# A decode block on one core: the first load issued in two parts, and seven transfers of rows in place of eight

## The chip, the cores and the metric

The kernel runs on one core of a Trainium2 chip. The metric is the device time of one execution in microseconds (us). The kernel before has a median of 213.9 us over three runs (213.82 to 213.99).

One execution was also recorded by the hardware profiler, and the profile shown here is of that one. Its engines are TensorE (PE, with its weight loads as PEld), VectorE (DVE), ScalarE (ACT), GpSimd (POOL) and SyncE (SP). SP does no arithmetic here: it issues transfers. A "q" behind an engine's name (SPq, ACTq) marks its instruction sequencer, which is what issues a transfer.

## The reference: attention over a cache, then a two-layer network

The block is one decode step for four tokens (B = 4) of width D = 448. What is computed, cut to what matters:

```python
def _A_ref(x, k_cache, v_cache, wq, wo):            # 16 query heads, 8 key heads, head size 256
    W = min(4096, max(256, Sk // 4))                # the last 1024 of 4096 cached positions
    q = (x @ wq).reshape(B, Sq, Hq, Dh) ...
    k = jnp.repeat(k_cache[:, :, Sk - W:, :], rep, axis=1)
    v = jnp.repeat(v_cache[:, :, Sk - W:, :], rep, axis=1)
    scores = jnp.einsum("bhqd,bhkd->bhqk", q, k) * (Dh ** -0.5)
    p = _softmax(scores, axis=-1)
    o = jnp.einsum("bhqk,bhkd->bhqd", p, v)
    return o ... @ wo
def _B_ref(x, w1, b1, w2, b2):                      # 448 -> 1792 -> 448
    y = _layernorm(x, axis=-1)
    h = _gelu(jnp.einsum("bsd,df->bsf", y, w1) + b1)
    return jnp.einsum("bsf,fd->bsd", h, w2) + b2

h = x + _A_ref(_layernorm(x, axis=-1), A_k_cache, A_v_cache, A_wq, A_wo)
h2 = h + _B_ref(_layernorm(h, axis=-1), B_w1, B_b1, B_w2, B_b2)
```

All data is float32. The keys and values of the last 1024 positions, for 8 heads and 4 tokens, are most of the 88 MB that are read from HBM.

## The kernel before

**Layout and staging.** The host packs everything that belongs together into arrays of 128 rows, one row for each SBUF partition, so that one transfer fills one stretch of all 128 partitions. Three large buffers form a ring (`slot`, line 50). The transfers fill them in turn: `t0` (first head), then `ta`, `tb`, `tc`, `td` for heads 0 to 2 and again for heads 3 to 5, and `te0` to `te2` for the last heads and the weights of the second layer. A buffer is filled again as soon as the work on its former content is done; that wait stands at the issue of the transfer.

**Who issues.** SP issues every load of these arrays, in program order, through `load` (line 53; the issue is on line 57). A load without a list of pieces is one transfer. ACT issues the small transfers of `rows` into the tile `rs` (lines 302 and 319). The three engines PE, SP and ACT run in the order in which the kernel's text names their instructions; nothing reorders them.

**The start.** Lines 259 to 267 issue the first loads: `wq0` (the query weights of head 0 and the transposed `x`: 128 rows of 7232 bytes) into the beginning of `t0`, then `k0` (keys of head 0 and most of the query weights of head 1) behind it, then two small transfers of 32 rows of 2048 bytes each into `wq1_last` (line 265). After these SP goes on to `ta` and `tb`. Lines 268 to 276 compute the first layer norm from `xT`, which lies in the `wq0` part; line 277 projects the first query; line 279 computes the first scores, which need `k0`.

**The rows.** The tile `rs` holds `x` and the two biases for the second half of the block. They are laid out in four groups of four partitions (0, 32, 64 and 96 onward), and for each group the kernel before issues two transfers, 256 columns and 448 columns wide (1 KB and 1.75 KB on each partition): four transfers at line 302 for groups 0 and 1, four at line 319 for groups 2 and 3. The first use of `rs` is line 400, near the end.

**The end.** The last loads are the pieces of `w2` (line 337). Line 463 multiplies with the first of them, line 473 with the rest, line 479 adds up, and line 480 writes the result.

Of the kernel before, what the change touches and what calls it, by code (L numbers as in the profile page):

```python
# [15 lines left out]
B, D = 4, 448  # L16
# [4 lines left out]
P = 128  # L21
H = P // 2
ND = 4
NKC = W // P
NFC = F // P
FQ = F // 4
# [3 lines left out]
WEIGHTS = 4 * D  # L30
# [5 lines left out]
def block_kernel(ctx: ExitStack, tc, rows, wq0, k0, wq1, la, lb, lc, ld, k7, vo, w1, w2, out):  # L36
    nc = tc.nc
# [12 lines left out]
    def slot(name):  # L50
        return ring.tile([P, SLOT], F32, tag="r", name=name)

    def load(t, at, src, pieces=None):
        dst = t[:, at : at + src.shape[-1]]
        at = 0
        for n in pieces or (src.shape[-1],):
            nc.sync.dma_start(dst[:, at : at + n], src[:, at : at + n])  # L57
            at += n
        return dst

    def cut(t, sizes):
        parts, at = [], 0
        for n in sizes:
            parts.append(t[:, at : at + n])
            at += n
        return parts


    def wq_parts(t, last=None):
        parts = [(a, yT[:, a, :], slice(0, 512), t[:, a * 512 : (a + 1) * 512]) for a in range(3)]  # L70
        if last is not None:
            return parts + [(3, yT[:H, 3, :], slice(0, 512), last)]
        for i in range(2):
            parts.append((3, yT[:, 3 + i, :], slice(i * 2 * P, (i + 1) * 2 * P), t[:, 3 * 512 :]))
        return parts


    def keys(t):
        return t.rearrange("p (c b k) -> p c b k", c=2, b=B)

    def chunks(t):
        v = t.rearrange("p (c b d) -> p c b d", b=B, d=DH)
        return [v[:, c : c + 2] for c in range(0, v.shape[1], 2)]
# [65 lines left out]
    def project_q(g, parts):  # L149
        pq = ps_m.tile([P, 512], F32, tag="m", name=f"pq{g}")  # L150
        for j, y, cols, w in parts:
            nc.tensor.matmul(pq[j * Q : (j + 1) * Q, cols], y, w, start=True, stop=True)  # L152
        qs = work.tile([P, 512], F32, tag="qs", name=f"qs{g}")
        nc.scalar.copy(qs, pq)  # L154

        pt = ps_m.tile([P, 2 * REP, P], F32, tag="m", name=f"pqt{g}")
        for i in range(2 * REP):
            nc.tensor.transpose(pt[:, i, :], qs[:, i * P : (i + 1) * P], ident)  # L158
        sm = work.tile([P, 2 * REP, B], F32, tag="sm", name=f"sm{g}")
        nc.vector.tensor_reduce(  # L160
            sm, pt.rearrange("p i (j q) -> p i q j", j=4)[:, :, :B, :], axis=AX.X, op=ALU.add
        )

        src = sm.rearrange("p (r c) b -> p c b r", r=REP)
        for i in range(2):
            nc.vector.tensor_copy(qT[g % 2][:, :, :, i * REP : (i + 1) * REP], src)

    def scores_half(g, h, kt):
        s = ps_s.tile([P, 512], F32, tag="s", name=f"s{g}_{h}")
        for c in range(2):  # L170
            for b in range(B):
                nc.tensor.matmul(  # L172
                    s[b * Q : (b + 1) * Q, :], qT[g % 2][:, c, b, :], kt[:, c, b, :],
                    start=(c == 0), stop=(c == 1),
                )
        m = work.tile([P, 1], F32, tag=f"mx{h}", name=f"mx{g}_{h}")
        nc.vector.reduce_max(m, s, axis=AX.X)  # L177
        return s, m

    def softmax(g, parts):  # L180
        halves, mx = zip(*parts)
        nm = work.tile([P, 1], F32, tag="nm", name=f"nm{g}")
        nc.vector.tensor_max(nm, mx[0], mx[1])
        nc.vector.tensor_scalar_mul(nm, nm, -SCALE)  # L184
        p = once.tile([P, 2 * 512], F32, tag="p", name=f"p{g}")
        sums = work.tile([P, 2], F32, tag="sums", name=f"sums{g}")
        for h in range(2):
            nc.scalar.activation(  # L188
                p[:, h * 512 : (h + 1) * 512], halves[h], AF.Exp, bias=nm, scale=SCALE,
                accum_out=sums[:, h : h + 1],  # L190
            )
        rec = work.tile([P, 1], F32, tag=f"rec{g % 3}", name=f"rec{g}")
        nc.vector.tensor_add(rec, sums[:, 0:1], sums[:, 1:2])
        nc.vector.reciprocal(rec, rec)
        return p, rec

    def scores(g, kt):
        return [scores_half(g, h, kt[h]) for h in range(2)]

    def transpose_p(g, p):  # L200
        for h in range(2):
            pt = ps_t.tile([P, 4, P], F32, tag="t", name=f"ppt{g}_{h}")
            for c in range(4):
                nc.tensor.transpose(pt[:, c, :], p[:, (4 * h + c) * P : (4 * h + c + 1) * P], ident)  # L204

            src = pt.rearrange("p (c i) (b q) -> p c i b q", i=2, b=B)
            for i in range(2):
                nc.vector.tensor_copy(
                    pT[g % 2][:, 2 * h : 2 * h + 2, :, i * REP : (i + 1) * REP], src[:, :, i, :, :REP]
                )  # L210


    def values(g, vt, po, pairs=range(NKC // 2)):
        for c in pairs:
            for b in range(B):
                nc.tensor.matmul(  # L216
                    po[b * Q : (b + 1) * Q], pT[g % 2][:, c, b, :], vt[c][:, :, b, :],
                    start=(c == 0), stop=(c == NKC // 2 - 1),
                )
# [35 lines left out]
    def po_tile(g, pool=ps_o, tag="o"):  # L255
        return pool.tile([P, 2, DH], F32, tag=tag, name=f"po{g}")


    t = slot("t0")
    wqt, xT = cut(load(t, 0, wq0), (WEIGHTS, ND * B))  # L260
    wqt = wq_parts(wqt)
    xT = xT.rearrange("p (a b) -> p a b", a=ND)
    ka, kb, wqt1 = cut(load(t, WEIGHTS + ND * B, k0), (HALF, HALF, 3 * 512))
# [17 lines left out]
    p, rec = softmax(0, parts)  # L281
    transpose_p(0, p)

    def finish(g, po, rec, wt):
        transposed_output(g, po, rec)
        add_output(g, output_weights(wt))

    for g in (0, 3):
        ka, kb, wqt, va = cut(load(slot(f"ta{g}"), 0, la[g // 3]), (HALF, HALF, WEIGHTS, HALF))
        parts = scores(g + 1, [keys(ka), keys(kb)])  # L290
        project_q(g + 2, wq_parts(wqt))
        p, rec_next = softmax(g + 1, parts)
        transpose_p(g + 1, p)
        po = po_tile(g)
        va = chunks(va)
        values(g, va, po, range(0, 2))

        vb, wot, ka, kb = cut(load(slot(f"tb{g}"), 0, lb[g // 3]), (HALF, WEIGHTS, HALF, HALF))
        if g == 0:
            for j in range(2):  # L300
                for cols in (slice(0, 2 * P), slice(2 * P, 2 * P + FQ)):
                    nc.scalar.dma_start(rs[j * Q : j * Q + B, cols], rows[j][:, cols])
        values(g, va + chunks(vb), po, range(2, 4))
        p, rec_then = softmax(g + 2, scores(g + 2, [keys(ka), keys(kb)]))
        finish(g, po, rec, wot)
        transpose_p(g + 2, p)

        wqt, v, wot, ka = cut(load(slot(f"tc{g}"), 0, lc[g // 3]), (WEIGHTS, CACHE, WEIGHTS, HALF))
        project_q(g + 3, wq_parts(wqt))
        po = po_tile(g + 1)  # L310
        values(g + 1, chunks(v), po)
        first_half = scores_half(g + 3, 0, keys(ka))
        finish(g + 1, po, rec_next, wot)

        kb, wqt, v, wot = cut(load(slot(f"td{g}"), 0, ld[g // 3]), (HALF, WEIGHTS, CACHE, WEIGHTS))
        if g == 0:
            for j in range(2, 4):
                for cols in (slice(0, 2 * P), slice(2 * P, 2 * P + FQ)):
                    nc.scalar.dma_start(rs[j * Q : j * Q + B, cols], rows[j][:, cols])
        parts = [first_half, scores_half(g + 3, 1, keys(kb))]  # L320
        project_q(g + 4, wq_parts(wqt))
        p, rec = softmax(g + 3, parts)
        transpose_p(g + 3, p)
        po = po_tile(g + 2)
        values(g + 2, chunks(v), po)
        finish(g + 2, po, rec_then, wot)
# [11 lines left out]
    p, rec_last = softmax(g + 1, scores(g + 1, kt))  # L338
# [122 lines left out]
    for c in range(first):  # L461
        j, m = c % 4, Q if c < 4 else B
# [90 lines left out]
```

## Time and profile before

| What | Value |
|---|---|
| median of 3 runs | 213.9 us (213.82 to 213.99) |
| profiled execution, its own time | 213.97 us |
| its span, first to last instruction | 212.2 us |
| read from HBM | 88.26 MB, 416 GB/s over the span |
| PE busy | 133.4 us (63% of the span) |
| DVE, ACT, POOL busy | 38.4, 21.2, 5.6 us |
| transfers of SP's queue (q1) | 3248 packets, 88.29 MB |
| transfers of ACT's queue (q10) | 64 packets, 0.05 MB |

The profiled execution took 213.97 us, of which 1.8 us lie outside its span; it stands 0.07 us above the median. Times within the span are counted from the first instruction. A packet is one row of a transfer on one of the core's 16 DMA engines, or the 4-byte write that ends a transfer on an engine. The view by windows counts a packet, with all its bytes and all its time, in the window in which it starts, so that single windows can show more than the whole rate.

### The profile page before, as it was taken

The page shows a single profiled execution, that of the slowest core. Times are in us where ns is not written, and L with a number is a line of the kernel's source. Part 1 is how long each engine was busy: PE and PEld are TensorE (multiplying, and loading weights), DVE is VectorE, ACT ScalarE, POOL GpSimd, SP SyncE. Part 2 cuts the span into 40 slices and gives each one's busy share as a digit, 9 for nine tenths or more (in the row PEclk, how much of TensorE's full clock was granted, in tenths as well). Part 3 has the DMA queues.
Part 4 walks back from the last instruction along what each step waited for, and adds up shares of the span by engine and source line. Part 5 has one row for each costly group of instructions (what it writes and reads, how often), then busy time and mean ns, then how long its engine had stood idle before and what let it go on. Part 6 is the DMA issues. An engine that isn't in the chain of part 4 may idle for free.

```text
span 212.2 us, 2296 instructions
## 1 busy us (share of the span) xinstructions
PE 133.4 (63%) x970; PEld 47.1 (22%) x970; DVE 38.4 (18%) x167; ACT 21.2 (10%) x52; POOL 5.6 (3%) x17
## 2 busy tenths in 40 slices
PE   0457815841960597188398088138917879978994
PEld 0322201310220221032123022012202322324432
DVE  1420310410230003022014013100200323122310
ACT  2010300300020100030003002001000302010311
POOL 6100000000000000000000000000000000000200
PEclk9999995995896559579969759855885999999999
DMA  7999898999999999999999999999989999999992
GB/s 292 426 396 534 350 499 361 481 416 467 397 419 482 407 420 420 467 393 457 428 425 467 422 407 482 407 431 407 479 349 463 442 399 424 432 393 439 424 398 77
DMA packets 3321, 88.46 MB, mean 417 GB/s; under 512 B 400, under 2 KB 688, under 8 KB 1392
## 3 DMA queue, kind: packets, MB, share of 16 engines
q1 hardware_dynamic: 3248, 88.29, 97.1%
q8 instruction: 7, 0.11, 0.2%
q10 hardware_dynamic: 64, 0.05, 0.1%
q14 instruction: 2, 0.02, 0.0%
HBM read 88.26 MB, written 0.07 MB: 416 GB/s over the span
## 4 chain that ended last, share of the span: by engine, by line
DMA 78%; PE 16%; SPq 2%; DVE 1%; issue 1%; ACT 1%; ACTq 0%
DMA tb<-lb 23%; DMA ta<-la 21%; DMA td<-ld 20%; DMA te<-w 14%; PE s L172 6%; PE po L216 4%; SPq L57 2%; PE ppt L204 1%; PE acc L245 1%; PE pq L152 1%; PE pa L463 1%; PE py L473 1%; SPq L265 1%; PE pqt L158 1%; ACT qs L154 1%
## 5 line engine op out<-in xcount | busy, mean ns | idle before, releaser
L177 DVE TENSOR_REDUCE mx<-s 128x1 f32<-128x512 f32 x16 | 11.1, 691 | 56.1 <-PE s L172 56.1
L172 PE MATMUL s<-ta,qT 128*32 128x512 f32 x64 | 10.7, 830 | 10.1 <-DMA ta<-la 10.1
L154 ACT COPY qs<-pq 128x512 f32<-128x512 f32 x8 | 4.7, 585 | 116.2 <-PE pq L152 116.2
L188 ACT ACTIVATE p<-s,nm 128x512 f32<-128x512 f32 x16 | 10.9, 688 | 46.4 <-DVE nm L184 46.4
L233 DVE TENSOR_SCALAR o<-po,rec 128x512 f32<-128x512 f32 x8 | 6.0, 750 | 50.5 <-PE po L216 50.5
L216 PE MATMUL po<-tb,pT 128*32 128x512 f32 x32 | 6.9, 1019 | 12.9 <-DMA tb<-lb 12.9
L152 PE MATMUL pq<-tc,yT 128*32 128x512 f32 (+1 forms) x20 | 3.9, 891 | 16.8 <-DMA tc<-lc 16.8
L172 PE MATMUL s<-td,qT 128*32 128x512 f32 x32 | 6.9, 1016 | 10.7 <-DMA td<-ld 10.7
L216 PE MATMUL po<-tc,pT 128*32 128x512 f32 x64 | 11.9, 909 | 0.0
L204 PE MATMUL ppt<-ident,p 128*128 128x128 f32 x64 | 10.5, 287 | 0.7 <-ACT p L188 0.4
L158 PE MATMUL pqt<-ident,qs 128*128 128x128 f32 x32 | 6.6, 340 | 6.0 <-ACT qs L154 6.0
L204 PEld LDWEIGHTS ppt<-ident,p 128*128 128x128 f32 x64 | 6.7, 141 | 6.3 <-ACT p L188 6.3
L160 DVE TENSOR_REDUCE sm<-pqt 128x16 f32<-128x64 f32 x8 | 1.8, 224 | 34.4 <-PE pqt L158 34.4
L216 PE MATMUL po<-te,pT 128*32 128x512 f32 x64 | 7.5, 595 | 0.6 <-DMA te<-vo 0.6
L172 PE MATMUL s<-tb,qT 128*32 128x512 f32 x64 | 7.4, 601 | 0.0
L216 PE MATMUL po<-td,pT 128*32 128x512 f32 x64 | 7.3, 595 | 0.0
L237 PE MATMUL pot<-ident,o 128*128 128x128 f32 x32 | 5.3, 287 | 2.7 <-DVE o L233 2.7
L345 PE MATMUL warm<-idle 128*32 128x512 bf16 x22 | 6.8, 382 | 0.0
L158 PEld LDWEIGHTS pqt<-ident,qs 128*128 128x128 f32 x32 | 4.2, 169 | 11.4 <-ACT qs L154 9.7
L172 PE MATMUL s<-t,qT 128*32 128x512 f32 x32 | 5.3, 829 | 2.0 <-DMA t<-k 2.0
L172 PEld LDWEIGHTS s<-ta,qT 128*32 128x32 f32 x64 | 2.6, 147 | 17.5 <-issue 13.5
L146 POOL TENSOR_TENSOR r<-ve_r,mhalf 128x1 f32<-128x1 f32 x2 | 1.1, 542 | 190.3 <-DVE ve_r L145 190.3
(129 smaller groups left out, 112.1 us busy)
## 6 DMA issues: line engine op xcount, KB each, us to landing
tc<-lc SPq DMA_DIRECT2D x2, 7936.0 KB
td<-ld SPq DMA_DIRECT2D x2, 7936.0 KB
ta<-la SPq DMA_DIRECT2D x2, 7040.0 KB
tb<-lb SPq DMA_DIRECT2D x2, 7040.0 KB
te<-vo SPq DMA_DIRECT2D x1, 4992.0 KB
t<-k SPq DMA_DIRECT2D x1, 4864.0 KB
te<-k SPq DMA_DIRECT2D x1, 4096.0 KB
te<-vo SPq DMA_DIRECT2D x1, 3072.0 KB
```

Of the source, the lines that this page charges most:

```text
L57: nc.sync.dma_start(dst[:, at : at + n], src[:, at : at + n])
L152: nc.tensor.matmul(pq[j * Q : (j + 1) * Q, cols], y, w, start=True, stop=True)
L154: nc.scalar.copy(qs, pq)
L158: nc.tensor.transpose(pt[:, i, :], qs[:, i * P : (i + 1) * P], ident)
L172: nc.tensor.matmul(s[b * Q : (b + 1) * Q, :], qT[g % 2][:, c, b, :], kt[:, c, b, :], start=(c == 0), stop=(c == 1),)
L177: nc.vector.reduce_max(m, s, axis=AX.X)
L188: nc.scalar.activation(p[:, h * 512 : (h + 1) * 512], halves[h], AF.Exp, bias=nm, scale=SCALE, accum_out=sums[:, h : h + 1],)
L204: nc.tensor.transpose(pt[:, c, :], p[:, (4 * h + c) * P : (4 * h + c + 1) * P], ident)
L216: nc.tensor.matmul(po[b * Q : (b + 1) * Q], pT[g % 2][:, c, b, :], vt[c][:, :, b, :], start=(c == 0), stop=(c == NKC // 2 - 1),)
L233: nc.vector.tensor_scalar_mul(o, po, rec)
L237: nc.tensor.transpose(pt[:, i, c], o[:, i, c * P : (c + 1) * P], ident)
L345: nc.tensor.matmul(warm[:Q], idle[:, :Q], idle, start=True, stop=True)
```

## The change

The first load is issued as two transfers, rows 0 to 31 and then rows 32 to 127, both into the same place as before. The tile, its layout and the bytes are the same, and so is everything that reads it. In the fourth group of `rows` one transfer of 704 columns takes the place of the two of 256 and 448 columns. The number of transfers in the whole kernel stays as it was: one more on SP, one fewer on ACT.

```diff
     t = slot("t0")
-    wqt, xT = cut(load(t, 0, wq0), (WEIGHTS, ND * B))
+    for p in (slice(0, 32), slice(32, P)):
+        nc.sync.dma_start(t[p, : WEIGHTS + ND * B], wq0[p])
+    wqt, xT = cut(t[:, : WEIGHTS + ND * B], (WEIGHTS, ND * B))
     wqt = wq_parts(wqt)
...
         if g == 0:
             for j in range(2, 4):
-                for cols in (slice(0, 2 * P), slice(2 * P, 2 * P + FQ)):
+                for cols in ((slice(0, 2 * P), slice(2 * P, 2 * P + FQ)) if j < 3 else (slice(0, 2 * P + FQ),)):
                     nc.scalar.dma_start(rs[j * Q : j * Q + B, cols], rows[j][:, cols])
```

## The prediction

> **What bounds the kernel now.** The page comes first: the span, the transfers by slice, their queues, and the chain that ended last.
>
> ```profile
> span 212.2 us, 2296 instructions
> ...
> DMA  7999898999999999999999999999989999999992
> ...
> q1 hardware_dynamic: 3248, 88.29, 97.1%
> ...
> q10 hardware_dynamic: 64, 0.05, 0.1%
> ...
> DMA 78%; PE 16%; SPq 2%; DVE 1%; issue 1%; ACT 1%; ACTq 0%
> ```
>
> The 16 DMA engines are busy from the second slice to the last but one; SP's queue alone takes 97.1% of them. Missing time is seen only in the first slice (0.7) and in the last (0.2). So the kernel ends when the stream of loads ends, plus a tail. Two things move the end: how soon the stream gets going, and how fast it runs. Compute that ends earlier or later inside the stream moves nothing, unless it starves the queue.
>
> The start, from the view of instructions in order of time, shows the issues and the compute that waits for them:
>
> ```profile
> 0.73 0.38 SPq L57 DMA_DIRECT2D t<-wq  x1
> 1.17 0.41 SPq L57 DMA_DIRECT2D t<-k  x1
> 1.62 1.55 SPq L265 DMA_DIRECT2D wq_last<-wq  x2
> 3.21 0.46 SPq L57 DMA_DIRECT2D ta<-la  x1
> 3.72 0.44 SPq L57 DMA_DIRECT2D tb<-lb  x1
> ...
> 5.57 0.57 PE L131 MATMUL pm_x<-t,mean 128*128 128x12 f32 x2 [5.57 <-DMA t<-wq]
> ...
> 15.49 0.25 DVE L166 COPY qT<-sm 128x16 f32<-128x16 f32 x2
> 17.20 5.34 PE L172 MATMUL s<-t,qT 128*32 128x512 f32 x32 [2.01 <-DMA t<-k]
> ...
> 23.45 0.33 SPq L57 DMA_DIRECT2D tc<-lc  x1
> ```
>
> The first load is waited for until 5.57. The query it leads to is in place at 15.49 + 0.25 = 15.74, and the first scores start at 17.20 because the keys land only then: 1.4 us of slack. SP issues five more loads by 4.16, and nothing after them until 23.45.
>
> What that queue holds is seen in the chain of work in order of time:
>
> ```profile
> 3.72 48.23 DMA tb<-lb
> 51.95 0.04 issue
> 51.99 3.30 PE po L216 x16
> ...
> 176.52 29.10 DMA te<-w
> 205.62 0.14 issue
> 205.76 1.71 PE pa L463 x16
> 207.47 0.72 PE py L473 x18
> ```
>
> The loads issued by 4.16 keep the engines busy until 51.95, so the issue at 23.45 has 28 us to spare. The chain's last load lands at 205.62, and its PE work starts 0.14 later; at that end a shift of the stream is a shift of the kernel.
>
> The stream's pace, from the view by windows (the last two numbers are the busy share of the DMA engines and GB/s):
>
> ```profile
> 1.73:2.73 1.00, 0.00 (x0) 0.00 (x0) 0.00 (x0) 0.28 (x1) 1.00 (x5) 1.00 0.87 166
> 2.73:3.73 1.00, 0.00 (x0) 0.00 (x0) 0.00 (x0) 0.00 (x0) 1.00 (x3) 1.00 0.97 405
> 16.20:16.36 0.16, 0.00 (x0) 0.00 (x0) 0.00 (x0) 0.00 (x0) 0.00 (x0) 1.00 0.54 205
> 210.62:210.93 0.31, 0.00 (x0) 0.00 (x0) 0.00 (x0) 0.00 (x0) 0.00 (x0) 1.00 0.70 210
> ```
>
> The first load's first microsecond has engines busy at 0.87 but moves 166 GB/s: a cold start. The next moves 405. From 16.20 to 16.36 only small packets start; the view of the queues for that window says which:
>
> ```profile
> DMA packets 19, 0.03 MB, mean 205 GB/s; under 512 B 3, under 2 KB 3, under 8 KB 19
> ```
>
> Nineteen less three completions are sixteen rows of 2048 bytes, those of the two 32-row transfers. A busy share of 0.54 of 16 is between eight and nine engines. This is the one place in the trace where 32 partitions are written in bulk, and they take 205 GB/s.
>
> **The change part by part.**
>
> *One more issue on SP.* An issue there costs 0.38 to 0.46 us with its step to the next (1.17 - 0.73 = 0.44). The issues behind it (`k0`, the 32-row pair, `ta`, `tb`) come 0.44 later. They are covered: `k0` is then issued at 1.61, and the engines have first-load rows until after 4 us (0.93 MB from 1.73: 0.17 MB in the first microsecond, 0.76 MB at 405 GB/s in 1.9 us more). With that cover gone it would cost 0.44. The second part's own issue is 0.44 behind the first's; the first part, 0.23 MB, needs about 1.0 + 0.07/0.405 = 1.2 us at the present pace, so it too is covered. Cost 0.
>
> *One more completion on each engine.* q10 has 64 packets (eight transfers of four rows, so half are completions); they take 0.1% of the 16 engines, at most 0.15% x 212.2 x 16 = 5.1 engine-us, or 0.08 each; the lower end is 0. I take 0.02.
>
> *One more landing for the first matmul to wait for.* Behind it on PE stands only the first layer norm and query, which have the 1.4 us of slack. The wait itself is priced by the chain's "issue" pieces, 0.04. Cost 0 while the first load lands less than 1.4 us later; above that it delays scores, still 28 us ahead of need.
>
> *Seven transfers of rows.* ACT issues one transfer fewer, and one completion and one packet go on each of four engines:
>
> ```profile
> 72.79 1.29 ACTq L319 DMA_DIRECT2D rs<-rows  x4
> 93.81 0.59 ACT L154 COPY qs<-pq 128x512 f32<-128x512 f32 x1 [20.45 <-PE pq L152]
> ```
>
> 1.29 / 4 = 0.32 us less on ACT, which then idles 20.45 us for PE: no gain. The rows are first used at line 400, near the end. On the DMA engines it saves at most two packets, 0.16, on four of sixteen, and the end waits for all sixteen: 0.
>
> *The pace of the 32 rows.* This is the unknown: no row shows 16 engines writing into 32 partitions. The part is 32 x 7232 bytes = 231 kB. At 405 GB/s it takes 0.57 us; at 205, the nearest row, 1.13: 0.56 more. How much the cold start hides is the bracket. It moves 166 kB in its first microsecond anyway, slower than 205. If it stays so, only the other 65 kB are held up, 65/205 - 65/405 = 0.16. So 0.16 to 0.56 where the limit holds, and 0 where 205 is only what eight engines can do. I take the middle of the limited case, 0.36.
>
> *The pace of the 96 rows.* 694 kB, 1.71 us at 405. Three times 205 is 615, over 405: by that no loss. But six rows to each engine, in order, would set two thirds of the engines on the upper 64 partitions, and if that half took no more than the 205 shown, its 463 kB would need 2.26 us: 0.55 more. Between 0 and 0.55 I take 0.15, nearer to the end that the row gives directly.
>
> *A quicker start.* The first row follows the issue by 1.73 - 0.73 = 1.00, while the result's transfer, 128 rows too, needed less:
>
> ```profile
> 209.77 0.35 SPq L480 DMA_DIRECT2D out<-res  x1
> ```
>
> Its rows move from 210.62 (the last window above), 0.85 behind. A shorter part could bring 0.15, and if it did away with the cold start, (405 - 166) kB / 405 = 0.59 more: 0.74 is the most it can gain. Nothing shows that the count of rows is the cause, as 128 rows started in 0.85 there, so I take 0.
>
> The sum is 0.36 + 0.15 + 0.02 = 0.53. Against the profiled execution's 213.97 that is 214.5; the median stands 0.07 lower, so the forecast is 214.4.
>
> The nearest row for the 32 rows is 205 GB/s. The Trainium skill, page SBUF — State Buffer, section on Door 1 and the DMA port swizzle, says that bandwidth follows from the number of ports that the partitions reach: partitions 0 to 31 reach eight of sixteen, about 218 GB/s, and 64 to 127 the other eight. The 205 stays below its 218 and doesn't contradict it, though with eight engines it doesn't test it. As an estimate from that page the 32 rows would cost 231/218 - 231/435 = 0.53 and the 64 upper rows 463/218 - 694/435 = 0.53, in all 1.06 instead of my 0.51, giving 215.0.
>
> **The rivals.**
>
> *Both parts at the full price (slower, more).* Nothing of the 32 rows' loss is hidden and the upper half is held too: 0.56 + 0.55 + 0.02 = 1.13, 215.0 on the median. For it: the engines never idle later, so a lost start is never made up. Against it: the cold start is slower than the limit. The page named above would give about the same.
>
> *No difference.* 205 GB/s is what eight engines carry, sixteen would carry twice that, and the parts follow each other without a gap: 213.9, from -0.15 to +0.3. For it: at 0.54 of the engines 205 is 380 at full share. Against it: those packets are a quarter as long, and eight engines are no test. In the Trainium skill, page DMA: Bandwidth & Descriptors, rules for kernel authors, it stands that two transfers to disjoint halves of the partitions just run one after the other, as they share the same engines; no run here shows such a pair yet.
>
> *Faster.* The cold start is that of a queue being filled with 128 rows, and 32 get all engines going at once. Half of the 0.74 is 0.37, 213.5. It decides if the first microsecond moves over about 166 + 0.53 x 405 = 380 kB, enough for the other terms as well. For it: the first slice is the one place with time to win. Against it: the result's 128 rows.
>
> *An issue waits for a landing it has nothing to do with.* The view of SP's waits shows one:
>
> ```profile
> SPq L57 <- DMA rs<-rows: 10.9, 1, 10.9
> ```
>
> The order of transfers is shifted by one between the first load and the fourth group of rows, so other pairs could wait. But SP's first waiting issue has 28 us to spare and ACT idles 20 us behind line 319. About nothing; within "no difference".
>
> **How the numbers follow.** A difference of 0.2% (0.43 us) is about what a measurement of this kernel can tell from none. Chances: the forecast, 214.4 (its own range 214.1 to 214.8), 0.33; full price, 215.0, 0.16; no difference 0.26; faster, 213.5, 0.25. The forecast's case lies over the 0.43 for the most part, so slower 0.46, within 0.29, faster 0.25. The range goes from 213.4, which holds over half of the faster case, to 215.1, the full price: about 0.15 is left out.
>
> **What would show it.** SP: two issues `t<-wq` 0.44 apart, and `k0` at 1.6. The windows from 1.73: if the forecast holds, the second microsecond falls well under 405 GB/s; if the faster case holds, the first rises over 380. Line 131 then starts near 6.1, not at 5.57, and the chain's last load lands about 0.5 later than 205.62, with the PE work behind it (from 205.76) unchanged in length. The prediction is wrong if the stream's later slices change: a slice under 8, or another spread at the end, would mean that the order of rows on the engines matters more than the start.

## The result, and the profile after

The changed kernel takes 215.18 us (median of six runs, 215.15 to 215.58), the kernel before 213.87 beside it. The ratio is 1.0062, 95% interval 1.0051 to 1.0072: 1.31 us, or 0.6%, slower. The profiled execution took 215.15 us, 1.18 more than the one of before.

The page of the changed kernel, with the lines that answer to those of before:

```profile
span 213.4 us, 2297 instructions
...
DMA  7998999999999999999999999999989999999991
...
q1 hardware_dynamic: 3264, 88.29, 97.1%
...
q10 hardware_dynamic: 56, 0.05, 0.1%
...
DMA 78%; PE 16%; SPq 2%; DVE 1%; issue 1%; ACT 1%; ACTq 0%
```

Nothing here gives the loss away. The engines are as busy as before (97.1% for SP's queue), the chain has the same shares, and the packets differ by the sixteen completions more on q1 and the eight packets fewer on q10. The start does show it, in the instructions in order of time:

```profile
0.73 0.85 SPq L261 DMA_DIRECT2D t<-wq  x2
...
1.62 0.43 SPq L57 DMA_DIRECT2D t<-k  x1
...
6.61 0.57 PE L131 MATMUL pm_x<-t,mean 128*128 128x12 f32 x2 [6.61 <-DMA t<-wq]
...
16.05 0.25 DVE L166 COPY qT<-sm 128x16 f32<-128x16 f32 x2
18.10 6.02 PE L172 MATMUL s<-t,qT 128*32 128x512 f32 x32 [2.35 <-DMA t<-k]
...
25.02 0.33 SPq L57 DMA_DIRECT2D tc<-lc  x1
```

The first load lands 1.04 us later (6.61 against 5.57), the keys 0.90 later (18.10 against 17.20). The query is ready at 16.30, still before the keys. In the chain of work the same shift goes through to the end:

```profile
4.17 49.02 DMA tb<-lb
53.23 3.64 PE po L216 x16
...
178.28 28.58 DMA te<-w
206.99 1.71 PE pa L465 x16
```

The `tb` load ends at 53.19 instead of 51.95 and the last load of the chain at 206.86 instead of 205.62: 1.24 us both times. So the whole loss is made before `tb` has landed, 1.04 of it before the first matmul, and the stream carries it to the end. The view by windows shows the pace at which it is lost; last are the busy share of the DMA engines and GB/s:

```profile
1.73:2.73 1.00, 0.00 (x0) 0.00 (x0) 0.00 (x0) 0.28 (x1) 1.00 (x5) 1.00 1.03 260
2.73:3.73 1.00, 0.00 (x0) 0.00 (x0) 0.00 (x0) 0.00 (x0) 1.00 (x3) 1.00 1.06 289
3.73:4.73 1.00, 0.00 (x0) 0.00 (x0) 0.00 (x0) 0.00 (x0) 0.31 (x1) 1.00 1.02 268
```

The first microsecond moved 260 GB/s against 166. That can't be credited to the cut: in the runs below that start with this load whole, the same microsecond moved 159 (`ta_rows`) to 253 (`ta_halves`). But where the kernel before went on with 405, and those runs with 383 to 427, this one stays at 289 and 268, with engines that count as fully busy.

How long a row keeps its engine busy follows from the view of the queues, which gives the rows that start in a stretch and the share of the 16 engines that they take. First a stretch inside the first load before (3.10 to 4.30 us), then one inside the 96 rows after (3.10 to 5.00 us):

```profile
DMA packets 71, 0.51 MB, mean 428 GB/s; under 512 B 0, under 2 KB 0, under 8 KB 71
...
q1 hardware_dynamic: 71, 0.51, 101.4%
```
```profile
DMA packets 72, 0.52 MB, mean 274 GB/s; under 512 B 0, under 2 KB 0, under 8 KB 72
...
q1 hardware_dynamic: 72, 0.52, 101.3%
```

Before, a row of 7232 bytes takes 1.014 x 16 x 1.2 / 71 = 0.27 us. Of the 96 rows, one takes 1.013 x 16 x 1.9 / 72 = 0.43. Each engine has six of them, so they cost about 0.9 us.

### The profile page after: what moved, and what is told of

Read it like the earlier page. It is cut to its first block, busy times and chain, and to the rows that moved or that the text cites. A ratio compares the mean times of both kernels' runs of the same rounds, so it can differ in the third digit from the quotient of the medians.

```text
span 213.4 us, 2297 instructions
## 1 busy us (share of the span) xinstructions
PE 134.3 (63%) x970; PEld 47.3 (22%) x970; DVE 38.1 (18%) x167; ACT 21.2 (10%) x52; POOL 5.6 (3%) x17
## 3 DMA queue, kind: packets, MB, share of 16 engines
q1 hardware_dynamic: 3264, 88.29, 97.1%
## 4 chain that ended last, share of the span: by engine, by line
DMA 78%; PE 16%; SPq 2%; DVE 1%; issue 1%; ACT 1%; ACTq 0%
DMA tb<-lb 23%; DMA ta<-la 21%; DMA td<-ld 20%; DMA te<-w 13%; PE s L172 6%; PE po L216 4%; SPq L57 1%; PE ppt L204 1%; PE pq L152 1%; PE acc L245 1%; PE pa L465 1%; PE py L475 1%; SPq L267 1%; PE pqt L158 1%; ACT qs L154 1%
## 5 line engine op out<-in xcount | busy, mean ns | idle before, releaser
L172 PE MATMUL s<-ta,qT 128*32 128x512 f32 x64 | 11.3, 874 | 9.2 <-DMA ta<-la 9.2
L216 PE MATMUL po<-tc,pT 128*32 128x512 f32 x64 | 9.5, 747 | 0.0
L172 PE MATMUL s<-tb,qT 128*32 128x512 f32 x64 | 8.1, 648 | 0.0
L172 PE MATMUL s<-t,qT 128*32 128x512 f32 x32 | 6.0, 921 | 2.3 <-DMA t<-k 2.3
```

What stands on the lines that cost most here:

```text
L172: nc.tensor.matmul(s[b * Q : (b + 1) * Q, :], qT[g % 2][:, c, b, :], kt[:, c, b, :], start=(c == 0), stop=(c == 1),)
L216: nc.tensor.matmul(po[b * Q : (b + 1) * Q], pT[g % 2][:, c, b, :], vt[c][:, :, b, :], start=(c == 0), stop=(c == NKC // 2 - 1),)
```

## The experiments

**Which half of the change it is.** One run has the split alone (`split_only`), one the seven transfers of rows alone (`rows_only`); their edits are the two hunks of the diff above.

> Only the first load is split (rows 0 to 31, rows 32 to 127); the rows of x and biases keep their eight transfers, so that every later transfer comes one later in the order. Theory A (the two parts write to only some of the partitions at a time, and 16 engines on part of the partitions are slowed): the whole loss is here, 1.1 to 1.5 us over before, 215.0 to 215.4. Theory B (it is the number and order of transfers, or the seven transfers of rows): another time than 215.2 by more than 0.4 us.

> Only the seven transfers of rows; the first load is whole. Theory A: no difference, 213.7 to 214.1. Theory B (part of the loss lies in the rows or in the order of transfers behind them): 214.3 or more.

The split alone took 215.35 us, ratio 1.0070 (1.0055 to 1.0085). The rows alone took 213.98, ratio 1.0005 (0.9995 to 1.0014). The loss is the split's, and the rows and the order of transfers behind them are worth nothing that can be measured.

**Two transfers, or rows?** Every run from here on has the seven transfers of rows.

```diff
-    wqt, xT = cut(load(t, 0, wq0), (WEIGHTS, ND * B))
+    wqt, xT = cut(load(t, 0, wq0, (452, 1356)), (WEIGHTS, ND * B))       # columns
...
+    for p in (slice(0, H), slice(H, P)):                                # halves, H = 64
+        nc.sync.dma_start(t[p, : WEIGHTS + ND * B], wq0[p])
```

> The first load is issued in two parts, as in the changed kernel, but each part has all 128 rows: columns 0 to 451 and 452 to 1807, a quarter and three quarters of the bytes; seven transfers of rows. Theory A (what costs is that a part covers only some partitions): 213.7 to 214.3, the first matmul at 5.4 to 5.8. Theory C (what costs is a second transfer, its issue and its completion, or the cold start met twice): as the changed kernel, 214.8 to 215.4, the first matmul after 6.3.

> The first load in two parts of rows 0 to 63 and 64 to 127; seven transfers of rows. Theory A with all 16 engines on one half of the destination at a time (both parts at 205 to 225 GB/s throughout): the first matmul at 6.3 to 6.9 and 215.0 to 215.4, as with 32 and 96 rows, although the cut is elsewhere. Theory D (the loss comes from 96 rows, which sixteen engines share unevenly over the upper partitions, or from the 32 rows being only a quarter): 214.0 to 214.6, as 64 rows are four for each engine, and half as bad as a quarter.

Cut by columns: 214.12 us (213.83 to 215.78), ratio 1.0023 (1.0005 to 1.0042), and the first matmul at 5.38. Two transfers as such don't cost what the change costs; why single runs of this kernel reached 215.78 was not found. Cut in halves: 216.17 us, ratio 1.0113 (1.0096 to 1.0130), which is worse than either expectation. Its windows and its first matmul:

```profile
2.73:3.73 1.00, 0.00 (x0) 0.00 (x0) 0.00 (x0) 0.00 (x0) 1.00 (x3) 1.00 1.09 318
3.73:4.73 1.00, 0.00 (x0) 0.00 (x0) 0.00 (x0) 0.00 (x0) 0.31 (x1) 1.00 1.00 217
4.73:5.73 1.00, 0.00 (x0) 0.00 (x0) 0.00 (x0) 0.00 (x0) 0.00 (x0) 1.00 1.08 231
```
```profile
7.51 0.57 PE L131 MATMUL pm_x<-t,mean 128*128 128x12 f32 x2 [7.51 <-DMA t<-wq]
```

From the second of these windows on, the pace is about the 205 to 225 that theory A named. The time is longer for two reasons, which the trace's records of each packet (its start, time and size) show: the rows, the keys' first rows among them, keep each engine busy for 1.7 us more than before, and the first row starts at 2.08 rather than 1.73, as SP takes 0.57 us to issue 64 rows, against 0.38 for the whole load.

**The same cuts on a load eight times as large.** The first `ta` load, 7.21 MB, is issued behind the keys and the 32-row pair, with no cold start ahead of it, and a loss that goes with the bytes must stand out. The edit, with the rows or columns of each run:

```diff
-        ka, kb, wqt, va = cut(load(slot(f"ta{g}"), 0, la[g // 3]), (HALF, HALF, WEIGHTS, HALF))
+        t = slot(f"ta{g}")
+        n = 3 * HALF + WEIGHTS
+        for p in ((slice(0, 32), slice(32, P)) if g == 0 else (slice(0, P),)):
+            nc.sync.dma_start(t[p, :n], la[g // 3][p])
+        ka, kb, wqt, va = cut(t[:, :n], (HALF, HALF, WEIGHTS, HALF))
...
# ta_halves: slice(0, H), slice(H, P);  ta_even_odd: slice(0, P, 2), slice(1, P, 2)
# ta_cols: the columns slice(0, n // 4), slice(n // 4, n) of all rows
```

> The first load is whole; the first ta load (7.21 MB, issued fourth, with no cold start before it) is issued in two parts of all 128 rows, a quarter and three quarters of the columns; seven transfers of rows. Theory A (a part that covers only some partitions is slowed): no difference, 213.7 to 214.3. Theory C (a second transfer costs by itself): more than 214.5.

> As the column cut, but the first ta load is cut into rows 0 to 31 and rows 32 to 127. Theory A: the loss grows with the bytes. 1.80 MB at 218 GB/s take 8.3 us and 5.41 MB at 280 GB/s (about the pace of the second part in the changed kernel) 19.3, against 16.9 at 427 for the whole: 10.7 more; with 326 GB/s for the second part 8.0 more. So 221 to 226. Theory C, or a loss tied to the start of the queue: under 215.5.

> The first ta load in rows 0 to 63 and 64 to 127. Theory A at the 217 to 231 GB/s that the halves of the first load showed: 7.21 MB take 31 to 33 us instead of 16.9, 228 to 231. If a half is slowed only while something else is cold: under 216.

> The first ta load in even rows and odd rows: two transfers of 64 rows each, as many rows, bytes and packets as with the halves, but each spread over all 128 partitions. If it matters which partitions are covered (theory A1: groups of partitions share a way in): near before, 213.8 to 216. If it matters how many rows a transfer has (theory A2: 16 engines on 64 rows): as the halves, 228 to 231.

| cut of the first `ta` load | us | ratio (95% interval) |
|---|---|---|
| columns | 213.96 | 1.0004 (0.9994 to 1.0013) |
| rows 0 to 31 and 32 to 127 | 232.42 | 1.0864 (1.0841 to 1.0887) |
| rows 0 to 63 and 64 to 127 | 233.09 | 1.0895 (1.0872 to 1.0919) |
| even rows and odd rows | 213.94 | 1.0002 (0.9992 to 1.0012) |

The pace, in the view by windows. The stretch from 20 to 32 us, inside the `ta` load, for the kernel before and for the even and odd rows:

```profile
20.00:32.00 12.00, 6.35 (x40) 2.13 (x32) 2.87 (x13) 1.93 (x5) 0.00 (x0) 0.96 1.04 451
```
```profile
20.00:32.00 12.00, 6.19 (x40) 2.06 (x32) 2.87 (x13) 1.94 (x5) 0.00 (x0) 0.95 1.04 451
```

For the 32 and 96 rows the same stretch, and one inside the second part, the 96 rows alone:

```profile
20.00:32.00 12.00, 8.15 (x46) 2.58 (x36) 2.88 (x13) 1.94 (x5) 0.00 (x0) 1.00 1.06 225
36.00:48.00 12.00, 0.00 (x0) 0.00 (x0) 0.00 (x0) 0.00 (x0) 0.00 (x0) 0.50 1.07 225
```

For the halves, inside the second part:

```profile
36.00:48.00 12.00, 0.00 (x0) 0.00 (x0) 0.00 (x0) 0.00 (x0) 0.00 (x0) 0.50 1.10 225
```

The column counts whole rows by their start, so it steps: 451 is 96 rows of 56,320 bytes in 12 us and 225 is 48. The view of the queues gives the time of a row, for the kernel before (20 to 32 us), for the 96 rows and for the second half (36 to 48 us):

```profile
q1 hardware_dynamic: 96, 5.41, 104.0%
```
```profile
q1 hardware_dynamic: 48, 2.70, 107.2%
```
```profile
q1 hardware_dynamic: 48, 2.70, 110.4%
```

A row takes 1.040 x 16 x 12 / 96 = 2.08 us before, 4.29 among the 96 rows and 4.42 in the second half. On 16 engines that is 433, 210 and 204 GB/s: a little less than half.

And the first scores on `ta`, for the 32 and 96 rows and for the even and odd rows:

```profile
52.57 1.08 PE L172 MATMUL s<-ta,qT 128*32 128x512 f32 x4 [23.70 <-DMA ta<-la]
```
```profile
33.93 1.08 PE L172 MATMUL s<-ta,qT 128*32 128x512 f32 x4 [7.03 <-DMA ta<-la]
```

So the loss goes with the bytes, 18.5 us on 7.21 MB, and it depends on which rows, and so which partitions, a transfer covers, not on their number: 64 rows in a block cost 19.2 us, 64 rows spread over all 128 partitions cost nothing. The 96 rows run at 210 GB/s, hardly faster than 64 rows in a block. My expectation of 8.0 to 10.7 more was half the truth, mostly because it gave the 96 rows 280 to 326. One rival stays open: a block of rows is also a block of the array in HBM, and no run cuts one without the other.

In the Trainium skill, page SBUF — State Buffer, section on Door 1, partitions 0 to 31 reach the same eight ports as 0 to 63, 64 to 127 the other eight, and eight ports carry about 218 GB/s. The 204 of the halves and the full pace of the even and odd rows agree with it. The 96 rows don't: they reach ports of both sides, and by a count of ports they should have run faster than 210. It would follow if all sixteen engines worked on the rows of one side at a time. The packet records fit that, as each of the 96 rows took between 3.94 and 4.42 us and none the 2.08 of before, but they don't name the engine of a packet, so it isn't shown.

**Why only 1.3 us, when the bytes say two?** At 225 GB/s the 925 kB of the first load take 4.1 us; at the 416 of the whole stream before they take 2.2, so 1.9 should be lost. Two kinds of run ask what the head of the stream hides: a load of the same size cut late in the stream, and the first load cut behind the keys.

```diff
-    wo_last = output_weights(load(e[1], CACHE + WEIGHTS, vo[1][:, CACHE:]))
+    for p in (slice(0, 32), slice(32, P)):                  # wo_even_odd: slice(0, P, 2), slice(1, P, 2)
+        nc.sync.dma_start(e[1][p, CACHE + WEIGHTS : CACHE + 2 * WEIGHTS], vo[1][p, CACHE:])
+    wo_last = output_weights(e[1][:, CACHE + WEIGHTS : CACHE + 2 * WEIGHTS])
...
     t = slot("t0")                                          # k_first, k_first_rows
+    ka, kb, wqt1 = cut(load(t, WEIGHTS + ND * B, k0), (HALF, HALF, 3 * 512))
     wqt, xT = cut(load(t, 0, wq0), (WEIGHTS, ND * B))       # k_first_rows: rows 0 to 31, rows 32 to 127
...
-    ka, kb, wqt1 = cut(load(t, WEIGHTS + ND * B, k0), (HALF, HALF, 3 * 512))
```

> The first load is whole; a load of nearly its size late in the stream, the output weights of the last head (128 rows of 7168 bytes, 0.918 MB, no cold start), is issued as rows 0 to 31 and rows 32 to 127; seven transfers of rows. Theory A1 with the cold start hiding a part of the loss in the changed kernel: the full price here, 918/225 - 918/434 = 1.96 us, so 215.5 to 216.2. If the changed kernel's 1.3 us is the whole price of such a cut of 0.92 MB, without any cover: 215.0 to 215.4.

> The same late load in even rows and odd rows. Theory A1: 213.7 to 214.3. If a second transfer costs anything late in the stream, above 214.3, and that is to be taken off the price of the 32 and 96 rows there.

> The two first loads change places: the 4.98 MB of keys first, then the first load, whole; seven transfers of rows. The stream has the same bytes and its engines are never idle; the first query comes 11 us later, which the 28 us of slack at the issue of tc cover. 213.6 to 214.4; more would mean that the slack is not what the chain says, and it is the base for the next.

> The same order, and the first load, now behind the keys and so without the cold start, in rows 0 to 31 and rows 32 to 127. If the cold start hid about half of the loss in the changed kernel: 925 kB at 225 GB/s take 4.1 us instead of 2.1, 2.0 or more over the run with the keys first (up to 3.2, as in the late load). If the changed kernel's 1.2 to 1.3 is the whole price and the cold start hides nothing: 1.0 to 1.5 over it.

The late load in even and odd rows took 213.89 us, ratio 0.9998 (0.9988 to 1.0007). In 32 and 96 rows its four runs took 217.24, 219.59, 220.95 and 221.51 us, far over what I expected and too far apart for one price. The profiled execution is the 217.24, and its chain shows that this is no clean price: the late loads now gate PE, which then works to the end with almost no load to wait for.

```profile
174.19 18.91 DMA te<-vo
193.09 0.04 issue
193.14 1.11 PE po L216 x8
...
209.20 1.75 PE pa L465 x16
```

What the unprofiled runs lost beyond this one stays open.

The pair with the keys first is cleaner. Whole: 214.50 us, ratio 1.0027 (1.0015 to 1.0039), a little above what I expected. Cut: 217.79, ratio 1.0170 (1.0151 to 1.0190). That is 3.3 us for the same cut that costs 1.3 at the head. The pace in one stretch, first whole, then cut:

```profile
15.00:16.00 1.00, 0.00 (x0) 0.00 (x0) 0.00 (x0) 0.00 (x0) 0.00 (x0) 1.00 1.05 441
```
```profile
15.00:16.00 1.00, 0.00 (x0) 0.00 (x0) 0.00 (x0) 0.00 (x0) 0.00 (x0) 1.00 1.07 217
```

So the same cut costs 2.0 us less at the head. The packet records say where the price lies: the time that packets take, summed and divided by the 16 engines, uncut and cut, beside the loss of the profiled execution.

| cut into 32 and 96 rows | own rows, us | rows queued beside it | sum | loss |
|---|---|---|---|---|
| first load, at the head | 2.68 to 3.54 | +0.28 (keys) | 1.1 | 1.18 |
| first load, behind the keys | 2.19 to 3.93 | +1.05 (`ta`, the 32-row pair, the keys) | 2.8 | 3.50 |
| late load | 2.20 to 4.04 | +1.60 (the loads around it) | 3.4 | 3.27 |
| first `ta` load | 16.64 to 34.23 | +0.78 (`tb`) | 18.4 | 18.51 |

So a cut away from the head costs more than its bytes at 225 GB/s for two reasons: its rows take a little more than twice as long, and rows queued beside it are slowed too. About 0.7 us of the keys-first pair stays open. At the head the first 32 rows lose nothing: they take 0.92 us of each engine, against 1.03 before and 0.81 to 1.04 in the other runs that start with it whole. There the first row of each engine is slow anyway. That belongs to the place and not to the load: with the keys first it is the keys' first row that is slow, 2.26 us on average where the later ones take 1.44, and the first load's rows take 0.27 from the start. The other 96 rows take 2.62 us of each engine instead of 1.66. Why they lose less there than the 96 rows of a later load wasn't found.

**The first load spread over all partitions.**

```diff
+    for p in (slice(0, P, 2), slice(1, P, 2)):
+        nc.sync.dma_start(t[p, : WEIGHTS + ND * B], wq0[p])
```

> The first load in even rows and odd rows, two transfers of 64 rows that each cover all 128 partitions; seven transfers of rows. Theory A1 (a transfer that covers one group of partitions is held to 225 GB/s, a spread one is not): no loss, 213.5 to 214.3, the first matmul at 5.3 to 5.9. If the two-part issue at the very start costs something beside the pace: 214.5 to 216, as with the halves. If a shorter first part gets the queue going sooner once its pace is not held: under 213.5.

It took 215.70 us, ratio 1.0078 (1.0049 to 1.0106), with runs from 214.40 to 216.36; the profiled execution is the fastest, 214.40. There the pace is near that of before, and what shows is a slower issue:

```profile
0.73 1.22 SPq L261 DMA_DIRECT2D t<-wq  x2
1.99 0.59 SPq L57 DMA_DIRECT2D t<-k  x1
...
5.92 0.57 PE L131 MATMUL pm_x<-t,mean 128*128 128x12 f32 x2 [5.92 <-DMA t<-wq]
```

Two issues of 64 rows took 1.22 us and the next 0.59, against 0.85 and 0.43 for the changed kernel, and the first matmul is 0.35 later than before. The profiled loss of 0.43 is about that. Its first row starts at 2.10 rather than 1.73, and its rows take 0.34 us on average, as before (0.34), where the changed kernel's take 0.44: spread rows aren't held back at the head either. What the slower runs lost more wasn't profiled and stays open. No cut beat the kernel before.

## Why the prediction was wrong in size

The direction was right, and so was the mechanism: slower, because 16 engines on a part of the partitions are held back. The size was not: 215.18 lies 0.8 us over the forecast of 214.4 and just over the top of the range, 215.1. The nearest case was the rival with both parts at the full price, 215.0, which I had given 0.16; its sum is near, its halves (0.56 and 0.55) are not.

The row that the price came from was misread, and that 205 is so near the 204 to 210 of a held-back load is luck. The window counts only packets that start in it, so 0.54 doesn't mean that eight or nine engines worked. It means that the sixteen rows took 0.536 x 16 x 0.16 / 16 = 0.086 us each, 24 GB/s on one engine, near the 27 of a whole load (56,320 bytes in 2.08 us). The rows of that pair weren't held back there, as the rival "no difference" had it with its 380 at full share.


- **The pace of the 96 rows** is the step that failed. I took 0.15 us from 0 to 0.55, because three times 205 is 615 and so over 405. That scaling was wrong: 96 rows ran at 210 GB/s in `ta`, hardly faster than 64 rows in a block. At the head they cost 2.62 - 1.66 = 0.96 us of each engine, above my upper end too, since I let only the upper half of the partitions be slow.
- **The keys behind them** I had put at nothing: their rows take 0.28 us more of each engine. Together with the 0.96 that is about the 1.24 by which `tb` lands later.
- **The pace of the 32 rows**, 0.36 from 0.16 to 0.56, was 0: at the head they take no longer than the first 32 rows of a whole load. The two errors partly cancel in the time.
- **The cold start as a cover** was right, and larger than I had it: it hides the whole loss of the 32 rows.
- **A quicker start**, taken as 0, was right. The sign I had named for the faster case, over 380 GB/s, didn't come, and the 260 of the first microsecond is hardly above what whole first loads reached.
- **One more issue on SP, one more landing to wait for**: right. `k0` is issued at 1.62 (forecast 1.61), the query stands at 16.30 ahead of the keys at 18.10, and `tc` at 25.02 is far ahead of its need.
- **One more completion, seven transfers of rows**: right to what can be measured. The order of transfers cost nothing, as said.
- **What would show it**: the second microsecond falls well under 405, to 289, as forecast. Line 131 starts at 6.61 rather than near 6.1, and the chain's last load is 1.24 later rather than 0.5. No later slice fell, and the tail kept its length.

## What to carry to other kernels

A load that fills all 128 partitions shouldn't be cut into blocks of rows: cut by columns, or take every second row, since 64 rows in a block ran at 204 GB/s and 64 spread rows at full pace, 433. That is for a load inside the stream; as the first load the even and odd rows still took 215.70 us and the columns 214.12, so there no cut paid. When a rate was seen in one place, it may belong to the place and not to the number of rows, so it mustn't be scaled by that number. And a loss at the head of a stream may be part hidden: the same cut cost 1.3 us as the first load and 3.3 as the second. And a window's GB/s counts what starts in it: over the busy share, or by the time of one row, it says more.

## What was not expected of the hardware

The busy share of the DMA engines doesn't tell a slow stream from a fast one. In the windows of the `ta` load it is 1.06 at 225 GB/s and 1.04 at 451: an engine that is held back counts as busy. The column of GB/s shows it, and so does the time of one row.

The 96 rows from 32 on ran hardly faster than a block of 64 (4.29 us a row against 4.42), and rows of a whole load queued behind a held-back one were slowed with it: the first sixteen rows of `tb` took 2.86 us on average instead of 2.08.

SP took about 0.6 us to issue a transfer of 64 rows (1.22 for two), against 0.85 for 32 and 96 rows together and 0.38 for 128. The 128 rows of the keys right behind the 64 took 0.59 as well, so the number of rows alone doesn't set it.
